# Places in a hand-written instruction order: similarities, sums, the fourth load, the low parts and the routing's ranks

## The chip, the cores and the metric

The kernel runs on one core of a Trainium2 chip. The metric is the device time of one execution in microseconds (us); the time of a kernel is the median of its runs. TensorE is called PE below, VectorE DVE, ScalarE ACT, GpSimd POOL and SyncE SP, as the profile does.

## The reference, cut to what matters

```python
# attention: q, k, v are (4 batches, 8 heads, 768 rows, 64)
q_assign = argmax(q_n @ c_n.T)          # nearest of 16 centroids, of normalized rows
k_assign = argmax(k_n @ c_n.T)
scores = (q @ k.T) / 8, where q_assign == k_assign, else -1e9
attn = exp(scores - max) / sum
x = (attn @ v) as 3072 tokens x 512
# routed experts: 8 of them, 512 -> 1024 -> 512
do_compute = x @ w_skip > 0
e = argmax(x @ w_gate); gate = softmax(x @ w_gate)[e]
out = x + gate * (relu(x @ w1[e]) @ w2[e])   # where do_compute, else out = x
```

## The kernel before, in words

Attention runs over 16 pairs of heads: 4 batches by 4 pairs, each pair two heads side by side. The experts follow, 8 in turn. Attention ends at about 460 us of the span, and the change lies in it alone.

The order of attention's instructions is written out by hand. `tasks` (L328) gives every step of pair i a time, counted in slots from that pair's first score. A pair has 24 slots (NS), one for each block of scores: two halves hf, six blocks kt, two heads a. `steps` (L305) takes the steps of all pairs off one heap by time, 24i + t, and issues them in that order; a step that yields a number goes back on the heap later by it, and one that yields a tuple waits for that time of its own pair. Each engine then runs its own instructions strictly in that program order. PLAN (L48) holds the times; FIRST (L61) and LAST, END (L77) replace some of them for the first and the last pairs. A time such as -46.95 is slot 1.05 of the pair two before; what follows names times by their slot in the running pair.

One slot holds, on PE, a score block (`score` L629: two products, L635 and L636) and a block of another pair's row maxima (`smax` L581: one product L586, whose maximum is taken by DVE at L588). ACT takes the exponential of the score block (L638), POOL adds exponentials up (L644, L650). Three times in a pair PE stops that rhythm for a group of products with v (`avs` L652, line L661, 16 records). These groups stand at slots 1.6, 9.6 and 17.6; below they and what follows them up to the next group are stretch A, B and C. During a group DVE has no new maxima to take, so its other work is put there: the choice of centroids, the low parts, the output's scaling and the routing.

The steps that the change moves:

- `sims` (L485): four products (L492) of 32 columns each with the centroids, then `assign` (L522) on DVE: a 32x32 transposition (L525), and in `first_max` (L502) a maximum (L506), a comparison (L509), a product with weights (L514), a maximum (L517) and an equality (L519), then a second transposition (L532). A yield stands between each two.
- `sums` (L695): four products (L701) of 32 columns that sum the exponentials, evicted by ACT (L704), then `recip` (L708: three transpositions L713, reciprocals L718) and `xout` (L789: three transpositions L764, then a scaling by DVE, L769, or ACT, L786).
- `load` (L393): the DMA of q and k of a pair into one of two buffers (RAW, by i % 2), on SP's queue. The buffer's last readers are the DMAs of `copies_lo` (L453, issued at L457) of the pair two before. SP also issues `load_v`, `gate_weights`, the copies of `split_hi` (L436), the mask rows (L555), the outputs (L778) and the experts' weights (L1300).
- `split_hi` (L429, ACT) and `split_lo` (L438, DVE L443): the high and low part of q (t = 0) and k (t = 1); `copies_lo` sends the low parts on at slots 2.8 and 2.9.
- `route_slots` (L864): after each of batches 0 to 2 (pairs 3, 7, 11), on DVE in small steps, the rank of each token within its expert: `route_c` (L957) with rk, rank, hi, los (L970 to L981), two one-hot tables oht (L985) and hs (L989), `route_cum` (L1011), then two products rhs and an accumulation in `route_d` (L993), then `route_e` (L1019). SLOTS (L58) lists the 20 times at which its yields wait.

PSUM has eight banks. `take` and `give` (L381, L390) hand them round in the order in which they were given back, so PE can run ahead of DVE and ACT only until the next bank in that order is still being read.

Of the kernel before, what the change touches and what calls it, by code (L numbers as in the profile page):

```python
# [25 lines left out]
HP = H // 2  # L26
# [19 lines left out]


PLAN = {  # L48
    "load": -60.0, "load_v": -45.0, "weights": 72.0, "sims": -46.95, "assign": (-46.42, 0.02, 0.02, 0.02, (-38.41,), 0.02),
    "hi": (-38.405, -38.40), "masks": (-32.5, 0.12), "lo": (-30.38, -30.37), "copies": (-22.1, -21.2, -21.1),  # L50
    "smax": (-21.6, 1.0, -0.2), "mneg": (-9.2, 4.0), "mrows": ((-6.5, 0.2, 0.05), (9.62, 0.1, 0.05)),
    "av": 1.6, "oT": (0.35, 3.55), "sums": 33.06, "recip": 33.64, "xout": (33.66, 49.55, 41.55),
    "route": (33.45, 41.5, 65.5), "early": (85.4, 100.9),
}

GATES = (41.62, 41.63, 41.64, 41.65, 41.66, 49.66, 49.67, 49.68, 49.69, 49.7, 49.71, 50.5,
         53.16, 53.17, 53.18, 65.67, 65.68, 65.69, 65.7, 73.66, 73.67)
SLOTS = (65.71, 65.72, 65.73, 65.74, 73.7, 73.71, 73.72, 73.73, 73.74, 81.66, 81.67, 84.4, 84.6,  # L58
         89.67, 89.68, 97.66, 97.67, 97.68, 97.69, 97.7)
CODES = {89.67: 85.9, 89.68: 85.91}  # L60
FIRST = {  # L61
    0: {
        "load_v": -18.9, "sims": -20.0, "hi": (-19.9, -19.8, -19.7, -19.6), "assign": (-19.0, 0.1, 0.01, 0.01, 0.01, 0.01),
# [6 lines left out]
        "mneg": (-4.6, 6.6), "mrows": ((-3.8, 0.2, 0.05), (9.45, 0.1, 0.05)),  # L70
    },
    2: {
        "load": -62.0, "load_v": -37.0, "sims": -38.9, "assign": (-38.42, 0.02, 0.02, 0.02, (-30.38,), 0.02), "hi": (-36.2, -30.3), "lo": (-22.39, -22.38), "masks": (-26.0, 0.12), "smax": (-17.6, 0.97, 0.0), "mneg": (-6.4, 5.2),
    },
}

LAST = {"sums": 29.2, "recip": 31.5, "xout": (31.52, 49.55, 37.55)}  # L77
# [5 lines left out]
class Kernel:  # L83
# [779 lines left out]

    def route_slots(self, i, bt):  # L864

        early = i == self.npair - HP - 1
        wait = iter([(CODES.get(t, t) if early else t,) for t in SLOTS])
        yield from self.route_c(i, bt * KT, KT, wait)
        yield next(wait)
        yield from self.route_cum(KT, wait)  # L870
        yield next(wait)
        yield from self.route_d(i, bt * KT, KT, wait=wait)
        yield next(wait)
        yield from self.route_e(i, bt * KT, KT, wait)
# [657 lines left out]
```

## Time and profile before

| what | us |
|---|---|
| median of 3 runs (lowest, highest) | 651.13 (650.85, 651.25) |
| the profiled execution's own time | 649.98 |
| its span | 648.3 |
| PE busy | 624.1, 96% of the span |
| DVE busy | 505.9, 78% |
| ACT busy | 410.0, 63% |
| POOL busy | 365.9, 56% |

Busy time of PE is modelled and its products overlap, so 96% says only that PE seldom stands still. What one more product costs is read from the chain of work that ended last: there a block of score or maxima stands with the time by which it moves the next one on.

### The profile page before, as it was taken

What the parts mean: (1) busy time and instruction counts of PE and PEld (TensorE: products, weight loads), DVE (VectorE), ACT (ScalarE), POOL (GpSimd) and SP (SyncE); (2) the same over time, 40 slices, a digit from 0 to 9 for tenths busy, and PEclk for the clock granted to TensorE, in tenths of its full rate; (3) what the DMA queues carried; (4) which work ended last, traced back from release to release, by engine and by line L of the source; (5) the groups of instructions that cost most, each with busy time, mean ns of one, the idle gap of its engine ahead of it and who ended that gap; (6) DMA issues with size and microseconds to landing.
All of it is one profiled execution on the core that took longest, in us unless ns stands there. A gap on an engine that the chain in (4) does not pass through costs nothing.

```text
span 648.3 us, 12165 instructions
## 1 busy us (share of the span) xinstructions
PE 624.1 (96%) x3873; PEld 460.5 (71%) x3873; DVE 505.9 (78%) x1060; ACT 410.0 (63%) x885; POOL 365.9 (56%) x384
## 2 busy tenths in 40 slices
PE   7879999999999999999999999999999999999994
PEld 3656776776667757767767666656799899899793
DVE  7967887888989869988888897885789766765721
ACT  7375787787767867867777777843654644645520
POOL 8784787777857867868777778631143212121101
PEclk9898999999999999999999999999999999999998
DMA  7396657776676565655754642341395766765711
GB/s 214 92 226 156 187 161 195 214 220 185 196 191 196 151 162 161 183 142 152 206 157 122 183 104 63 97 146 52 116 330 169 273 221 235 225 206 188 235 45 36
DMA packets 54322, 110.09 MB, mean 170 GB/s; under 512 B 8600, under 2 KB 22808, under 8 KB 54257
## 3 DMA queue, kind: packets, MB, share of 16 engines
q1 hardware_dynamic: 51232, 101.92, 54.2%
q0 software_dynamic: 2624, 7.18, 3.3%
q8 instruction: 32, 0.52, 0.3%
q14 instruction: 34, 0.27, 0.1%
q10 hardware_dynamic: 400, 0.20, 0.1%
HBM read 60.93 MB, written 10.55 MB: 110 GB/s over the span
## 4 chain that ended last, share of the span: by engine, by line
PE 67%; DMA 13%; issue 9%; DVE 8%; POOL 1%; ACT 1%; SPq 0%; POOLq 0%; DVEq 0%; ACTq 0%
PE ps L661 17%; PE ps L635 10%; PE ps L586 9%; PE ps L636 9%; DMA out<-yo,idw 7%; DMA raw<-qk 3%; DVE M L588 2%; PE ps L492 2%; PE ps L701 2%; DMA xg<-out,idr 2%; PE ph L1066 2%; PE ph L1065 2%; PE ph L1064 2%; PE ps L764 1%; DVE raw L443 1%
## 5 line engine op out<-in xcount | busy, mean ns | idle before, releaser
L650 POOL TENSOR_TENSOR acc<-acc,PT 128x384 f32<-128x384 f32 x246 | 245.6, 1027 | 43.8 <-ACT PT L638 43.0
L588 DVE TENSOR_REDUCE M<-ps 128x1 f32<-128x384 f32 x384 | 197.7, 552 | 38.6 <-PE ps L586 38.1
L638 ACT ACTIVATE PT<-ps 128x384 f32<-128x384 f32 x384 | 180.1, 492 | 42.1 <-PE ps L636 31.2
L635 PE MATMUL ps<-D 102*128 102x384 f32 x384 | 136.9, 356 | 4.5 <-DVE M L588 3.8
L661 PE MATMUL ps<-PT,vt 128*64 128x385 f32 x768 | 135.7, 494 | 0.0
L586 PE MATMUL ps<-D 96*128 96x384 f32 x384 | 133.4, 355 | 1.0 <-ACT D L566 1.0
L636 PE MATMUL ps<-D 128*128 128x384 f32 x384 | 130.4, 340 | 0.0
L661 PEld LDWEIGHTS ps<-PT,vt 128*64 128x64 f32 x768 | 50.8, 136 | 63.0 <-issue 60.1
L635 PEld LDWEIGHTS ps<-D 102*128 102x128 f32 x384 | 73.2, 191 | 25.7 <-issue 7.2
L644 POOL TENSOR_TENSOR acc<-PT 128x384 f32<-128x384 f32 x64 | 55.0, 878 | 61.0 <-ACT PT L638 60.3
L586 PEld LDWEIGHTS ps<-D 96*128 96x128 f32 x384 | 73.5, 192 | 22.1 <-ACT PT L638 8.7
L1222 POOL DMA_INDIRECT out<-yo,idw x15 | 20.3, 1350 | 111.9 <-DVE yo L1098 101.9
L636 PEld LDWEIGHTS ps<-D 128*128 128x128 f32 x384 | 73.6, 192 | 0.0
L1350 ACT ACTIVATE hh<-ph 128x256 fp32r<-128x256 f32 x56 | 21.5, 384 | 46.4 <-PE ph L1066 46.4
L1351 DVE SCALAR_TENSOR_TENSOR hl<-ph,hh 128x256 fp32r<-128x256 f32 x56 | 23.7, 423 | 33.6 <-ACT hh L1350 33.4
L1322 ACT ACTIVATE D<-wraw 128x1024 fp32r<-128x1024 f32 (+1 forms) x45 | 44.1, 1002 | 6.3 <-PE py L1066 4.7
L1064 PE MATMUL ph<-x2l,D 128*128 128x256 f32 x168 | 47.7, 284 | 0.0
L1065 PE MATMUL ph<-x2h,D 128*128 128x256 f32 x168 | 47.5, 283 | 0.0
L1064 PE MATMUL py<-D,hh 128*128 128x512 f32 x112 | 45.0, 402 | 0.0
L621 ACT ACTIVATE D<-ps,blocks 6x256 fp32r<-6x256 f32 x84 | 33.3, 457 | 16.1 <-PE ps L610 15.7
L1323 DVE TENSOR_TENSOR D<-wraw,D 128x1024 fp32r<-128x1024 f32 (+1 forms) x29 | 34.3, 1184 | 6.3 <-ACT D L1322 5.6
L443 DVE TENSOR_TENSOR raw<-raw,D 128x768 fp32r<-128x768 f32 x28 | 35.9, 1310 | 0.1
(312 smaller groups left out, 1032.0 us busy)
## 6 DMA issues: line engine op xcount, KB each, us to landing
wraw<-w SPq DMA_DIRECT2D x72, 512.0 KB, 4.9
D<-D SPq DMA_DIRECT2D x124, 192.0 KB, 3.4
raw<-qk SPq DMA_DIRECT2D x16, 768.0 KB, 5.7
D<-raw SPq DMA_DIRECT2D x60, 192.0 KB, 3.4
vt<-v SPq DMA_DIRECT2D x16, 384.0 KB, 4.1
out<-x SPq DMA_DIRECT2D x31, 192.0 KB, 2.8
D<-mk SPq DMA_DIRECT2D x120, 24.0 KB, 1.9
out<-yo,idw POOLq DMA_INDIRECT x15, 4.9
```

The costliest lines, as they stand in the source:

```text
L443: eng.tensor_tensor(out=lo.bitcast(F32R), in0=lo, in1=c[f"hi{t}"].bitcast(F32), op=ALU.subtract)
L586: nc.tensor.matmul(sm, lhsT=c["qm"][a][0:96, j * P:(j + 1) * P], rhs=c["kb"][a][0:96, hf * HALF:(hf + 1) * HALF], start=True, stop=True)
L588: nc.vector.tensor_reduce(out=c["m"][:, j, a, hf:hf + 1], in_=sm, axis=AX.X, op=ALU.max)
L635: nc.tensor.matmul(ps, lhsT=c["kb"][a][:MR, ks], rhs=c["qm"][a][:MR, sl], start=True, stop=False)
L636: nc.tensor.matmul(ps, lhsT=c["kc"][a][:, ks], rhs=c["qc"][a][:, sl], start=False, stop=True)
L638: nc.scalar.activation(out=pt, in_=ps, func=AF.Exp, scale=D ** -0.5)
L644: nc.gpsimd.tensor_tensor(out=acc, in0=self.pt(i, s - 2)[:, :HALF], in1=pt, op=ALU.add)
L650: (nc.vector if dve else nc.gpsimd).tensor_tensor(out=acc, in0=acc, in1=pt, op=ALU.add)
L661: nc.tensor.matmul(av[a * D:(a + 1) * D, :], lhsT=c["vt"][:, kt, a * D:(a + 1) * D], rhs=self.pt(i, hf * 2 * KT + kt * 2 + a), start=(kt = ...
L1064: mm(ps, lhsT=ah, rhs=bl, start=first, stop=False)
L1065: mm(ps, lhsT=ah, rhs=bh, start=False, stop=False)
L1322: nc.scalar.activation(out=h[:, cs], in_=r[:, cs], func=AF.Copy)
```

## The change

Nothing is added to the computation or taken from it; entries of the order are placed anew.

- `sims` goes from slot 1.05 to 1.52 (for pairs 3 to 15) and from 9.1 to 9.54 (pair 2): behind the maxima block of slot 1.2 (9.4 for pair 2), which stood between it and what follows.
- `sums` goes from slot 9.06 to 9.55, behind the maxima block of slot 9.4 (pairs 0 to 13; pair 14 has its own time).
- In `assign` the product with weights (L514) goes from stretch A to B for pairs 3 to 15, in front of the maximum L517. Pairs 0 to 2 keep their own lists.
- `split_lo` of k (t = 1) goes from slot 17.63, right behind that of q, to slot 1.62 of the next stretch A, for pairs 3 to 15.
- The load of pair 3 (the fourth) goes from slot 12 to slot 8 of the first pair.
- `route_slots`: rk, rank, hi and los go from stretch C to the next stretch A (65.71 to 73.69). After batches 0 and 1 the steps behind them move on too: oht, hs and cum from A to B, the second rhs from B to C, the accumulation from C's end to a later place in C, and the first two steps of `route_e` from C to A. After batch 2 those keep their places.

```diff
-    "load": -60.0, "load_v": -45.0, "weights": 72.0, "sims": -46.95, "assign": (-46.42, 0.02, 0.02, 0.02, (-38.41,), 0.02),
-    "hi": (-38.405, -38.40), "masks": (-32.5, 0.12), "lo": (-30.38, -30.37), "copies": (-22.1, -21.2, -21.1),
+    "load": -60.0, "load_v": -45.0, "weights": 72.0, "sims": -46.48, "assign": (-46.42, 0.02, 0.02, (-38.42,), 0.02, 0.02),
+    "hi": (-38.405, -38.40), "masks": (-32.5, 0.12), "lo": (-30.38, -22.38), "copies": (-22.1, -21.2, -21.1),
...
-    "av": 1.6, "oT": (0.35, 3.55), "sums": 33.06, "recip": 33.64, "xout": (33.66, 49.55, 41.55),
+    "av": 1.6, "oT": (0.35, 3.55), "sums": 33.55, "recip": 33.64, "xout": (33.66, 49.55, 41.55),
...
-SLOTS = (65.71, 65.72, 65.73, 65.74, 73.7, 73.71, 73.72, 73.73, 73.74, 81.66, 81.67, 84.4, 84.6,
-         89.67, 89.68, 97.66, 97.67, 97.68, 97.69, 97.7)
-CODES = {89.67: 85.9, 89.68: 85.91}
+SLOTS = ((73.69, 73.7, 73.71, 73.72, 81.67, 81.68, 81.69, 81.7, 81.71, 81.72, 89.66, 91.0, 91.2,
+          97.66, 97.67, 97.68, 97.69, 97.7, 97.71, 97.72),
+         (73.69, 73.7, 73.71, 73.72, 73.73, 73.74, 73.75, 73.76, 73.77, 81.66, 81.67, 84.4, 84.6,
+          85.9, 85.91, 97.66, 97.67, 97.68, 97.69, 97.7))
...
     2: {
-        "load": -62.0, "load_v": -37.0, "sims": -38.9, "assign": (-38.42, 0.02, 0.02, 0.02, (-30.38,), 0.02), "hi": (-36.2, -30.3), "lo": (-22.39, -22.38), "masks": (-26.0, 0.12), "smax": (-17.6, 0.97, 0.0), "mneg": (-6.4, 5.2),
+        "load": -62.0, "load_v": -37.0, "sims": -38.46, "assign": (-38.42, 0.02, 0.02, 0.02, (-30.38,), 0.02), "hi": (-36.2, -30.3), "lo": (-22.39, -22.38), "masks": (-26.0, 0.12), "smax": (-17.6, 0.97, 0.0), "mneg": (-6.4, 5.2),
     },
+    3: {"load": -64.0},
...
-        early = i == self.npair - HP - 1
-        wait = iter([(CODES.get(t, t) if early else t,) for t in SLOTS])
+        wait = iter([(t,) for t in SLOTS[i == self.npair - HP - 1]])
```

## Rows read from the trace of the kernel before

**Rows 1.** The page's first part: busy time, share of the span, instructions.
```profile
PE 624.1 (96%) x3873; PEld 460.5 (71%) x3873; DVE 505.9 (78%) x1060; ACT 410.0 (63%) x885; POOL 365.9 (56%) x384
```

**Rows 2.** Waits of PE, whole span: total us, times, longest us.
```profile
PE ps L492 <- DMA raw<-qk: 4.3, 2, 3.6
PE ps L635 <- DVE M L588: 3.8, 5, 1.1
```

**Rows 3.** Chain that ended last, 202 to 209 us, a stretch A: start, us, what.
```profile
203.13 0.78 PE ps L492 x8
203.92 0.38 PE ps L586
...
204.62 2.74 PE ps L661 x16
...
208.10 0.18 PE ps L635
```

**Rows 4.** The same chain, 209 to 219 us, the next stretch B.
```profile
211.63 0.78 PE ps L701 x8
212.41 0.37 PE ps L586
```

**Rows 5.** The same chain, 58 to 64 us: transpositions behind a group of v products.
```profile
62.43 0.48 PE ps L713 x3
62.91 0.33 PE ps L764 x3
```

**Rows 6.** The same chain, 0 to 66 us: the fourth load and what follows.
```profile
39.24 9.16 DMA raw<-qk
48.53 1.51 PE ps L492 x8
50.04 0.62 PE ps L586
50.66 3.36 PE ps L661 x16
```

**Rows 7.** Busy us of each engine by stretch; the figure behind POOL is PE's granted clock.
```profile
48.50:51.00 2.50, 2.47 (x11) 0.81 (x13) 0.30 (x1) 0.00 (x0) 0.00 (x0) 0.50 0.19 47
```

**Rows 8.** The DMAs of line L457, 28 to 45 us: issue times, and landing.
```profile
L457 SPq DMA_DIRECT2D D<-raw x4: 600/635/831, 32.2 to 34.5; - x4
...
DMA to landing us min/median/max: 3.8/4.0/4.3
```

**Rows 9.** The loads of line L396, 0 to 80 us: landing.
```profile
DMA to landing us min/median/max: 4.3/5.2/9.2
```

**Rows 10.** Timeline, 166 to 178 us, a stretch C with routing: start, us, engine, what.
```profile
169.24 2.63 DVE L443 TENSOR_TENSOR raw<-raw,D 128x768 fp32r<-128x768 f32 x2
...
173.16 0.20 DVE L970 TENSOR_TENSOR rk<-ps,ohd 128x48 f32<-128x48 f32 x1
...
174.04 0.91 DVE L981 SCALAR_TENSOR_TENSOR los<-hi,rank 128x6 f32<-128x6 f32 x1
...
175.47 0.45 PE L635 MATMUL ps<-D 102*128 102x384 f32 x1 [1.09 <-DVE M L588]
```

**Rows 11.** Timeline of DVE, 176 to 202 us, the stretches A and B behind it.
```profile
182.05 1.02 DVE L985 TENSOR_TENSOR oht<-iota,los 128x384 bf16<-128x384 f32 x2
...
183.33 0.62 DVE L1017 TENSOR_TENSOR cum<-cum,cs 128x8 bf16<-128x8 bf16 x1
...
190.24 0.77 DVE L999 TENSOR_TENSOR rhs<-rv,hs 128x240 bf16<-128x240 bf16 x2
...
191.22 0.27 DVE L718 RECIPROCAL rs<-ps 128x6 f32<-128x6 f32 x2 [0.20 <-PE ps L713]
```

**Rows 12.** Line L443, 166 to 260 us: duration ns min/median/max.
```profile
L443 DVE TENSOR_TENSOR raw<-raw,D x8: 947/1209/1762, 169.2 to 248.4; 128x768 fp32r<-128x768 f32 x8
```

**Rows 13.** Line L514, whole span: duration ns min/median/max.
```profile
L514 DVE TENSOR_TENSOR eqc<-eqc,wts x16: 552/557/560, 9.6 to 361.3; 128x384 f32<-128x384 f32 x16
```

**Rows 14.** Line L981, whole span: duration ns min/median/max.
```profile
L981 DVE SCALAR_TENSOR_TENSOR los<-hi,rank x5: 161/910/922, 174.0 to 446.8; 128x6 f32<-128x6 f32 x3, 128x3 f32<-128x3 f32 x2
```

## The prediction, made before the changed kernel was run

> **What bounds the kernel now.** I read the busy shares first: PE works 96% of the span [rows 1], so the question is what PE does with its time and where it stands still. The waits of PE answer the second part: it waits little, and two entries carry nearly all of it in attention, 4.3 us for a load of q and k (3.6 of it in one wait) and 3.8 us in five waits for DVE's maxima [rows 2]. The first part comes from the chain of work that ended last. In the steady rhythm it is PE's own stream, one product every 0.18 us [rows 3], so a slot of three products is 0.53 us. One thing breaks the stream beside the real work: a 128-column product that comes behind products of 32 columns moves the chain on by 0.38 or 0.37 us in place of 0.18 [rows 3, 4]. So PE is the bound, and a gain has to be a wait of PE or such a step; DVE matters only where it makes PE wait.
>
> **The fourth load.** The load of pair 3 is issued at 39.24 and lands 9.16 us later, at 48.40, and PE starts the similarities of pair 3 at 48.53 [rows 6], 3.57 of the 3.6 us wait [rows 2] after its previous product ended at 44.96. Behind the wait the granted clock is 0.50, that is 1.2 GHz [rows 7], after an engine that had stood still; the similarities take 1.51, the maxima block 0.62 and the v products 3.36 us [rows 6], against 0.78, 0.38 and 2.74 at full clock [rows 3], 1.59 us more. From 44.96 to the group's end at 54.02 are 9.06 us. With the load in time and the new order they are 0.18 + 0.78 + 2.74 = 3.70, so the whole wait is worth 5.4 us.
>
> Is it in time? The buffer is read by the low copies of pair 1; the last of the four is issued at 34.5 and lands at most 4.3 later, at 38.8 [rows 8]. Placed at slot 8, the load stands behind these copies on SP's queue and waits for that landing, so it is issued at 38.8 to 39.2, hardly sooner than now. What changes is what stands ahead of it: now two loads of v, the gate weights and two high copies are in flight, and 9.16 is the longest landing of five loads; the others take 4.3 to 5.2 and some more [rows 9]. I take 5.2, the median: landing at 44.0 to 44.4, against 45.1 when PE wants it. That is close, 0.7 us, and it is the step I trust least. Queued behind the waiting load on SP are the v loads of pairs 1 and 2 and the gate weights (wanted a stretch or more later) and the four high copies of pair 2, held for up to 3.6 us. Those are wanted by the first maxima of pair 2, some 2.4 us (4.4 slots) behind the v products, at 51; a stall of 0 to 1.5 us, of which I take 0.3. Sum: -5.0 us, between -5.4 and 0.
>
> **Sums.** Today they stand 32-column, 128-column (maxima), 64-column (v products), and the maxima block pays 0.37 [rows 4]. Behind the change the maxima block keeps the rhythm at 0.18 and the sums run straight into the v products. The v products take 2.74 behind a 128-column block, so entering column tiles shows no price. 14 pairs by 0.19 us = -2.7 us. The eviction L704 comes some 0.2 us later; nothing needs it before the transpositions behind the v products, 2.7 us on.
>
> **Similarities.** The same would hold, but in 12 of the 13 stretches A (pairs 4 to 15) three transpositions of `xout`, 128 columns wide, stand between slot 1.52 and the v products. Leaving column tiles then costs there: three transpositions behind v products take 0.48, three behind others 0.33 [rows 5], 0.15 more. So the gain is 0.20 - 0.15 = 0.05 by 12 = 0.6, and 0.2 for pair 2; that of pair 3 is in the load. -0.8 us. Bounds: 0.2 if the transpositions pay the full 0.20, and 12 by 0.20 + 0.2 = 2.6 if they pay nothing. The page TensorEngine Tiling (Array Packing) of the Trainium skill, Key Properties, says that a change of tiling mode drains PE; by it the number of changes in a stretch A is four before and four after, and this edit gives 0.2, not 0.8. The rows agree for leaving a mode and show no price for entering one.
>
> **The ranks and the low part, taken from stretch C.** There DVE works through two low parts (2.63 us), then the gates and, from 173.16 to 174.95, rk, rank, hi and los; the maxima come after that, and PE, having run out of free banks, waits 1.09 us [rows 10]. That wait stands once behind each of batches 0, 1 and 2, three of the five in [rows 2]. With one low part (1.3) and 1.8 us of ranks gone, DVE is free 3.1 us sooner, and nothing else is late: 3 by 1.09 = -3.3 us. In all other pairs stretch C makes PE wait for nothing and loses only a low part.
>
> **What that costs in stretches A and B.** In A the low part arrives, 0.95 to 1.76 us, median 1.21 [rows 12], and the product L514 leaves, 0.56 [rows 13]: about 0.65 more, and DVE gets its similarities some 0.5 sooner, since the maxima block is no longer behind them. The cover is the v products and, behind them, four slots that PE can run ahead on free banks, 2.74 + 4 x 0.53 = 4.9 us, and the list (transposition, maximum, comparison, low part, the first maxima) is some 3.5 us. No price in the pairs without routing. Behind batches 0 and 1, A gains the ranks too (0.7 to 1.8 us, as los takes 161 to 922 ns [rows 14]) but loses oht, hs and cum, from 182.05 to 183.95, 1.9 us [rows 11]; there the two small waits of PE that are left of the five, 0.5 us in all [rows 2], go or stay. I take them as gone, -0.5, with +1 as the other end. The GPSIMD Engine Reference of the Trainium skill, Specifications, says that GpSimd shares SBUF interfaces with VectorE; by it los is short where POOL is idle, as it is under v products, and the ranks cost 0.7 in A. The 161 and 922 of one small shape agree with that.
>
> B takes 0.56 (L514) in every pair: in front of it DVE waits for PE at the maxima block, which comes 0.6 sooner now; no price. Behind batches 0 and 1, B also takes oht, hs and cum, 1.9, and gives up one rhs of two, 0.4 [rows 11]: 0.56 + 1.9 - 0.4 = 2.1 us ahead of the reciprocals, whose bank PE wants two slots after the transpositions. Against it stand 0.2 us that DVE waits there now [rows 11], the 0.5 by which it starts sooner and two slots, 1.1: 1.8 in all. A stall of 0.3 by this, 0 to 1.9 by its ends; I take 0.5, twice: +1.0. One PSUM bank (rk's input) is held eight slots longer in three stretches; with six others left the rhythm needs no more.
>
> **Sum.** -5.0 - 2.7 - 0.8 - 3.3 - 0.5 + 1.0 = -11.3 us on the profiled execution's own 649.98, that is 638.7. The median of the runs lies 1.15 above that execution, so 639.8. PE's stream goes on to the end of the span, and nothing there is tied to a clock of its own, so I pass the whole of it on.
>
> **The rivals.**
> 1. The load is late all the same. For it: its issue hardly moves, and 9.16 is a landing that the trace shows. Against: that one had several transfers ahead of it. From 39 + 9.2 = 48.2 PE waits 3 us of the 3.6 again, clock included; the gain of the load is 0 to 1. Time 644 to 645. Chance 0.15.
> 2. Every switch of mode drains, entering too, as the tiling page has it: then similarities give 0.2 and the sums as forecast, 640.4. Chance 0.1. The opposite, where transpositions pay nothing and B shows no stall, is 637. Chance 0.07.
> 3. Slower: PE's run-ahead on free banks is not there in the steady pairs, and DVE's list decides stretch A. Place: the first maxima behind the v products; it decides from the point at which that list passes 4.9 us. Price: the low part in full (1.3) less L514 (0.56), 0.75, and L514 in B, 0.56, by 12 pairs = 15.7, with up to 3.8 in B behind routing; C gives nothing back, since PE doesn't wait there. With 12.3 of gains that is +7, 658. Against it: PE waits for DVE in no stretch A without routing now. Chance 0.05.
> 4. The order does not show: DVE's new waits eat what the switches give and the load is late: 650 to 652. Chance 0.04.
>
> **How the numbers follow.** Forecast 639.8, chance 0.59; with the parts of rival 2 the band 637 to 642 holds 0.76. The range goes from all terms at their better end (-5.4, -2.8, -2.6, -3.3, -0.5, no stall: 636.5) to a late load, 645.5. About 0.2% (1.3 us) is what a measurement of this kernel tells from none. Faster 0.91, same 0.04, slower 0.05.
>
> **What would show it.** Among PE's waits the load's 3.6 us is gone, and the clock's 0.50 behind it; the three waits of 1.1 for the maxima are gone. In the chain, L586 takes 0.18 in front of sums and similarities, L661 follows L701 directly, and the first transpositions behind L492 take about 0.48. Wrong it would be by a new wait: L492 or the first maxima of pair 2 on a DMA at 45 to 52 us, or L635 on DVE's reciprocals, scaling or maxima in A and B.

## The result, and the profile after

The changed kernel takes 642.74 us (median; 641.93 to 643.25) against 650.99: ratio 0.9872, interval 0.9855 to 0.9889. It is 8.2 us faster, inside the forecast range, where 11.3 us of gain were forecast. Its profiled execution has a span of 640.2 us against 648.3.

The lines of the kernel's code stand one or two lower than before (L637 is the former L635, L588 the former L586). First the changed kernel's busy shares and PE's waits for DVE from 40 us on; the columns are those of [rows 1] and [rows 2].

```profile
PE 619.7 (97%) x3873; PEld 459.1 (72%) x3873; DVE 504.1 (79%) x1060; ACT 409.3 (64%) x885; POOL 361.9 (57%) x384
```
```profile
PE ps L637 <- DVE M L590: 2.7, 1, 2.7
...
PE ps L588 <- DVE rs L720: 0.5, 2, 0.3
...
PE ps L637 <- DVE x L771: 0.5, 2, 0.2
```

The wait for the load is gone, and so are the five for the maxima, 3.8 us. In their place stands one wait of 2.7 us for the maxima, and four small ones for the reciprocals and the output's scaling. The steady stretches look as forecast. The chain of work that ended last, 288 to 335 us, a stretch A and then the next stretch B (start, us, what):

```profile
296.20 0.17 PE ps L588
296.38 0.78 PE ps L494 x8
297.16 0.48 PE ps L766 x3
...
304.64 0.17 PE ps L588
304.81 0.78 PE ps L703 x8
305.59 2.74 PE ps L663 x16
```

The maxima block L588 takes 0.17 where it took 0.38 and 0.37 [rows 3, 4]; the sums run straight into the v products; behind the similarities the transpositions take 0.48, not 0.33 [rows 5].

Where the time went is read from the starts of the v products in the two timelines, us:

```
group of v products                     before    after   difference
first                                    29.48    29.44    -0.04
third, behind the similarities of 3      50.59    45.79    -4.80
fourth                                   59.62    54.01    -5.61
batch 0: stretch C begins               169.00   162.44    -6.56
         stretch A begins               179.10   170.88    -8.22
         stretch B begins               187.78   178.84    -8.94
         next stretch C begins          196.06   187.89    -8.17
batch 2: stretch C begins               375.55   364.44   -11.11
         stretch A begins               384.68   371.95   -12.73
         stretch B begins               392.82   383.89    -8.93
         next stretch C begins          401.16   392.74    -8.42
end of the span                         648.28   640.17    -8.11
```

At 372 us the change is 12.7 us ahead, more than forecast. In the stretch A that follows batch 2 and in its wake it gives 4.3 of them back. PE and DVE there, from the timeline of the changed kernel (start, us, engine, what; in brackets idle time and what ended it):

```profile
372.20 1.59 DVE L445 TENSOR_TENSOR raw<-raw,D 128x768 fp32r<-128x768 f32 x1
373.72 0.97 DVE L951 CAST vals<-g 128x6 bf16<-128x6 f32 x1
...
375.63 0.17 DVE L982 SCALAR_TENSOR_TENSOR los<-hi,rank 128x6 f32<-128x6 f32 x1
375.83 1.70 DVE L986 TENSOR_TENSOR oht<-iota,los 128x384 bf16<-128x384 f32 x2
377.45 0.82 DVE L990 TENSOR_TENSOR hs<-iota,hi 128x12 bf16<-128x12 f32 x1
...
378.45 0.76 DVE L1018 TENSOR_TENSOR cum<-cum,cs 128x8 bf16<-128x8 bf16 x1
379.14 1.01 DVE L590 TENSOR_REDUCE M<-ps 128x1 f32<-128x384 f32 x2
...
379.74 0.44 PE L637 MATMUL ps<-D 102*128 102x384 f32 x1 [2.67 <-DVE M L590]
```

Between the last maxima of the stretch before (ended 372.28) and the first new ones (379.14) DVE has 6.9 us of low part, gate values, ranks and tables to do. The v products start at 371.95 and PE works through four slots behind them, to 377.1; then its banks are used up. The 6.9 us and 0.6 of the first new maxima, against the 4.8 from 372.28 to 377.07, make the wait of 2.67. The stretch 382 to 384 us shows the clock behind the wait at 0.50, 1.2 GHz (busy us by engine, then the granted clock):

```profile
382.00:384.00 2.00, 2.00 (x12) 0.33 (x13) 1.99 (x4) 0.51 (x2) 2.00 (x3) 0.50 0.00 0
384.00:387.00 3.00, 3.00 (x16) 1.11 (x16) 1.12 (x2) 2.38 (x3) 0.85 (x1) 0.84 0.03 5
```

### The profile page after: what moved, and what is told of

The parts are those of the page before. It is cut to its first block, busy times and chain, and to the rows that moved or that the text cites. A ratio compares the mean times of both kernels' runs of the same rounds, so it can differ in the third digit from the quotient of the medians.

```text
span 640.2 us, 12142 instructions
## 1 busy us (share of the span) xinstructions
PE 619.7 (97%) x3873; PEld 459.1 (72%) x3873; DVE 504.1 (79%) x1060; ACT 409.3 (64%) x885; POOL 361.9 (57%) x384
## 4 chain that ended last, share of the span: by engine, by line
PE 31%; DMA 10%; issue 9%; DVE 4%; ACT 0%; POOL 0%; POOLq 0%; DVEq 0%
DMA out<-yo,idw 7%; PE ps L663 6%; PE ps L637 4%; PE ps L638 3%; PE ps L588 3%; DMA xg<-out,idr 2%; PE ph L1066 2%; PE ph L1065 2%; PE ph L1067 2%; PE py L1066 1%; PE py L1065 1%; PE py L1067 1%; DVE M L590 1%; DMA PT<-out,idr 1%; PE ps L703 1%
## 5 line engine op out<-in xcount | busy, mean ns | idle before, releaser
L652 POOL TENSOR_TENSOR acc<-acc,PT 128x384 f32<-128x384 f32 x246 | 242.2, 1013 | 47.3 <-ACT PT L640 46.9
L637 PE MATMUL ps<-D 102*128 102x384 f32 x384 | 135.9, 354 | 3.9 <-DVE M L590 2.7
L588 PE MATMUL ps<-D 96*128 96x384 f32 x384 | 130.3, 346 | 2.2 <-ACT D L568 1.0
L637 PEld LDWEIGHTS ps<-D 102*128 102x128 f32 x384 | 72.8, 190 | 24.5 <-issue 6.6
L588 PEld LDWEIGHTS ps<-D 96*128 96x128 f32 x384 | 73.1, 191 | 6.3 <-ACT D L568 1.4
L1065 PE MATMUL py<-D,hh 128*128 128x512 f32 x112 | 45.0, 402 | 0.0
L623 ACT ACTIVATE D<-ps,blocks 6x256 fp32r<-6x256 f32 x84 | 33.3, 457 | 12.7 <-PE ps L612 12.3
L1066 PE MATMUL py<-D,hh 128*128 128x512 f32 x84 | 33.0, 392 | 0.0
```

The source lines that it names most:

```text
L588: nc.tensor.matmul(sm, lhsT=c["qm"][a][0:96, j * P:(j + 1) * P], rhs=c["kb"][a][0:96, hf * HALF:(hf + 1) * HALF], start=True, stop=True)
L637: nc.tensor.matmul(ps, lhsT=c["kb"][a][:MR, ks], rhs=c["qm"][a][:MR, sl], start=True, stop=False)
L652: (nc.vector if dve else nc.gpsimd).tensor_tensor(out=acc, in0=acc, in1=pt, op=ALU.add)
L1065: mm(ps, lhsT=ah, rhs=bl, start=first, stop=False)
L1066: mm(ps, lhsT=ah, rhs=bh, start=False, stop=False)
```

## The experiments

The differences in us inside a trace are differences of the starts of v products, as in the table above, against the changed kernel unless said otherwise. The kernel before ran beside each, and ratios are to it. All of them compute the whole result. Line numbers are each kernel's own: L493 of the kernel with the load back is L492 of the kernel before.

**The load back** (`load_back`).

```diff
-    3: {"load": -64.0},
```

> The changed kernel with the load of pair 3 back at slot 12, all else as changed. My account: the wait of PE for that load returns in front of L494 with the slow clock behind it, 5.3 us, so 648.0 (ratio 0.9955). Rival, that the load's wait was mostly covered by something else and the gain came from the order around it: less than 2 us, so under 644.7.

Measured: 647.95 us, ratio 0.9958 (0.9935 to 0.9982), against 0.9872 with the load moved. PE's wait is back:

```profile
PE ps L493 <- DMA raw<-qk: 3.1, 1, 3.1
```

The load lands 8.8 us behind its issue here (at 39.23) and 4.4 us behind it in the changed kernel (at 39.03). There SP issued nothing from 34.9 us up to the load; here it issued two loads of v, two of the gate weights and two high copies in that time. Up to 372 us this kernel is 4.8 us behind, so more than half of the 8.2 us that the change gives is this one transfer. A further 1.2 us come behind batch 2, where the clock stays low for longer behind the same wait (last section); that the median meets the expected 648.0 is in part chance.

**The load alone** (`load_alone`), in the kernel before.

```diff
+    3: {"load": -64.0},
```

> The kernel before with the load of pair 3 at slot 8 and nothing else. My account: PE's wait for it goes with its slow clock, 4.8 us (what putting it back cost in the trace) to 5.3: ratio 0.992, 645.9. Rival, that the load is only in time because the similarities of pair 3 stand later: some of the wait stays, 646.5 or more, and a wait of L492 for raw shows in the trace.

Measured: 644.98 us, ratio 0.9922 (0.9892 to 0.9953), 4.9 us in the trace by 60 us and unchanged to the end. No wait of L492 for raw is left. So the load doesn't need the later similarities.

**The sums back** (`sums_back`).

```diff
-    "sums": 33.55,
+    "sums": 33.06,
```

> The changed kernel with the sums back at slot 9.06, in front of the maxima block. My account: the maxima block pays the 0.19 us for leaving 32-column products again in 14 stretches B, 2.7 us, so 645.4 (ratio 0.9914), and PE's chain shows 0.37 for it. Rival, that PE's stream is not what sets the time in stretch B: under 1 us more, below 643.7.

Measured: 645.72 us, ratio 0.993 (0.9908 to 0.9951). The trace is 2.86 us behind at 372 us, near 14 x 0.19 = 2.7, and another 1.5 behind the wait of stretch A. That wait is 2.7 us here too, but the clock behind it stays low for longer (last section), so the 1.5 are not the sums'. The chain of this kernel, 300 to 312 us, shows the price where it was expected:

```profile
306.84 0.78 PE ps L703 x8
307.62 0.37 PE ps L588
307.99 2.74 PE ps L663 x16
```

**The similarities back** (`sims_back`).

```diff
-    "sims": -46.48, ...   (pair 2: -38.46)
+    "sims": -46.95, ...   (pair 2: -38.9)
```

> The changed kernel with the similarities back at slot 1.05 (9.1 for pair 2). My account: 0.05 us in each of 12 stretches A and 0.2 for pair 2 and for pair 3, 1.0 us, so 643.7 (ratio 0.989). Rival by the tiling rule, that each change of mode costs the same: 0.4 us, 643.1, within what can be told; the chain then shows the same sum of L494, L588 and the transpositions as in the changed kernel.

Measured: 644.59 us, ratio 0.992 (0.9891 to 0.9949); the trace is 2.73 us behind at 372 us, more than either account gives. 0.9 of it are small steps, about 0.05 in a stretch A and 0.5 by pairs 2 and 3 (0.3 of that stands at the first group already, where traces of kernels that are alike so far differ by up to 0.15): the chain, 290 to 300 us, has 0.38 + 0.33 behind L494 where the changed kernel has 0.17 + 0.48.

```profile
298.12 0.78 PE ps L494 x8
298.91 0.38 PE ps L588
299.28 0.33 PE ps L766 x3
```

The other 1.8 are three steps of 0.6, in the stretch A in which the gates of a batch are worked out, and there a wait shows that the changed kernel has not:

```profile
PE ps L588 <- DVE M L590: 1.0, 3, 0.4
```

Similarities behind the maxima let DVE start its list sooner, and in three stretches that decides whether PE waits. The kernel before has the similarities at the same early place and no wait there; its low part of k stands in stretch C, and with that moved alone a wait of 0.5 to 0.7 us comes there (`low_alone`). The forecast had the effect (0.5 us sooner) and no price for it.

**The tables behind batch 2 moved to stretch B** (`tables_to_b`).

```diff
-         (73.69, 73.7, 73.71, 73.72, 73.73, 73.74, 73.75, 73.76, 73.77, 81.66, 81.67, 84.4, 84.6,
+         (73.69, 73.7, 73.71, 73.72, 81.61, 81.62, 81.63, 81.64, 81.65, 81.66, 81.67, 84.4, 84.6,
```

> The changed kernel with oht, hs and cum behind batch 2 moved from stretch A (73.73 to 73.77) to stretch B (81.61 to 81.65). My account of the new wait of 2.67 us at 379.7: DVE's list there runs 6.9 us from the last maxima to the next ones, past the 4.9 us that the v products and four slots of run-ahead cover; without the tables (3.3 us) the list is 3.6 and the wait is gone with its slow clock, 4.2 us less: 638.5 (ratio 0.981), with up to 1 us of a new wait in stretch B. Rival, that PE lacks a PSUM bank since rk's input is held eight slots longer: the list is not the cause, the wait stays, 642.7.

Measured: 637.53 us, ratio 0.9799 (0.9773 to 0.9826). The wait of 2.7 us is gone from the list, which now has

```profile
PE ps L588 <- DVE rs L720: 0.6, 2, 0.3
PE ps L637 <- DVE x L771: 0.5, 2, 0.3
```

and the trace is 4.4 us ahead of the changed kernel. rk's input holds its bank as long as in the changed kernel, so the bank was not the cause.

**The last pair's low part back in stretch C** (`last_low_back`).

```diff
-END = {"mrows": ...
+END = {"lo": (-30.38, -30.37), "mrows": ...
```

> The changed kernel with the low part of k of the last pair alone back in stretch C. It takes 1.59 us out of DVE's list behind batch 2. By the list account the wait of 2.67 us falls to some 1.1, and with a shorter gap the clock may stay: 1.6 to 3 us less, 639.7 to 641.1. By the rival (a missing PSUM bank) nothing changes, 642.7.

Measured: 637.66 us, ratio 0.9804 (0.9778 to 0.9831); 4.1 us ahead in the trace, more than expected. 1.6 us less of work took 2.4 us off the wait, of which 0.3 is left. The rest of the list became 0.8 us shorter in sum: oht 1.03 where it took 1.70, hs 0.16 where it took 0.82 (below), against rv, 1.04 where it took 0.31.

```profile
374.78 1.03 DVE L986 TENSOR_TENSOR oht<-iota,los 128x384 bf16<-128x384 f32 x2
375.72 0.16 DVE L990 TENSOR_TENSOR hs<-iota,hi 128x12 bf16<-128x12 f32 x1
```

This run shows one thing more. In its stretch C behind batch 2 both low parts stand again and only the ranks are gone, and PE does not wait there: the starts around that stretch lose 0.1 us against the changed kernel.

```profile
364.54 2.62 DVE L445 TENSOR_TENSOR raw<-raw,D 128x768 fp32r<-128x768 f32 x2
...
368.46 3.80 DVE L590 TENSOR_REDUCE M<-ps 128x1 f32<-128x384 f32 x8
```

**The ranks and tables of all batches back** (`ranks_back`), the low part left where the change put it.

```diff
-SLOTS = ((73.69, 73.7, 73.71, 73.72, 81.67, 81.68, 81.69, 81.7, 81.71, 81.72, 89.66, 91.0, 91.2,
-          97.66, 97.67, 97.68, 97.69, 97.7, 97.71, 97.72),
-         (73.69, 73.7, 73.71, 73.72, 73.73, 73.74, 73.75, 73.76, 73.77, 81.66, 81.67, 84.4, 84.6,
+SLOTS = ((65.71, 65.72, 65.73, 65.74, 73.7, 73.71, 73.72, 73.73, 73.74, 81.66, 81.67, 84.4, 84.6,
+          89.67, 89.68, 97.66, 97.67, 97.68, 97.69, 97.7),
+         (65.71, 65.72, 65.73, 65.74, 73.7, 73.71, 73.72, 73.73, 73.74, 81.66, 81.67, 84.4, 84.6,
```

> The changed kernel with all of the routing's ranks and tables at their old times, and the low part of k where the change put it. It tells which of the two moves took the three waits of 1.09 us out of stretch C. If the low part alone does (1.3 us out of a list that overran by 1.1): no wait in C, the 2 x 0.8 us of new small waits in B gone, the wait behind batch 2 cut by the ranks' 0.75 us to 1.9: 642.7 - 1.6 - 0.8 = 640.3. If the ranks were needed: up to 3 x 1.1 us of waits in C return: 643.6.

Measured: 637.04 us, ratio 0.9811 (0.9776 to 0.9846), 5.0 us ahead of the changed kernel in the trace, of which 0.5 stands behind each of batches 0 and 1 and the rest behind batch 2. That is some 3 us better than expected: the wait behind batch 2 was put at 1.9 us, and 0.26 is left. Stretch C has no wait for the maxima at all: with one low part in front of them the ranks are done at 166.4 and the maxima go on at once (timeline of DVE, 160 to 180 us; before it was 174.95 in a stretch that began 6.6 us later).

```profile
166.27 0.17 DVE L982 SCALAR_TENSOR_TENSOR los<-hi,rank 128x6 f32<-128x6 f32 x1
166.35 3.85 DVE L590 TENSOR_REDUCE M<-ps 128x1 f32<-128x384 f32 x8
```

So the low part alone is enough to take the three waits out of stretch C, and with it moved, the move of the ranks and tables brought nothing there and cost 5 us. The kernel with the last pair's low part back shows the other half behind batch 2: there the ranks' move alone is enough.

**The low part alone** (`low_alone`), in the kernel before.

```diff
-    ... "lo": (-30.38, -30.37), ...
+    ... "lo": (-30.38, -22.38), ...
```

> The kernel before with the low part of k at slot 1.62 and nothing else. My account after the runs so far: this alone takes the three waits of 1.09 us out of stretch C, 3.3 us; in stretch A the product with weights stays too, so behind the routing up to 0.6 us of small waits come in each of three: 1.5 to 3.3 us less than the kernel before, 647.8 to 649.6 (ratio 0.995 to 0.9977). Rival, that the ranks have to leave stretch C as well: no gain, 651.

Measured: 658.53 us, ratio 1.0132 (1.0097 to 1.0166): slower by 1.3%, where both accounts had it at or below the kernel before. Stretch C does lose its wait, 1.6 us each time. But in stretch A the list is now longer than its cover: the product with weights L514 is still there, the similarities still stand in front of the maxima block, and behind each batch the tables stand there too:

```profile
PE ps L635 <- DVE M L588: 7.0, 6, 2.5
...
PE ps L701 <- POOL acc L650: 2.0, 3, 0.7
```

Against the kernel before, the stretch A of the gates loses 1.5 to 1.7 us in each of three batches and that of the tables 2.2 behind batch 0 and 4.8 behind batch 1. The step that takes three times 1.6 us out of stretch C is a net loss of 8 to 9 by itself. With the ranks back the tables and the low part share stretch A as well, and behind batches 0 and 1 that kernel loses only 0.5 us each time against the changed one. That leaves the later similarities and the move of L514 as what makes room for the low part; no run shows what L514 alone is worth.

**The output's transpositions in front of the similarities** (`out_first`).

```diff
-    "xout": (33.66, 49.55, 41.55),
+    "xout": (33.66, 49.5, 41.55),
```

> The changed kernel with the output's transpositions (L766) moved in front of the similarities (slot 1.55 to 1.50), so that 32-column products run straight into the v products in stretch A. My account: the first of three transpositions then no longer pays 0.15 us for leaving column tiles, 12 times, 1.8 us less: 641.0 (ratio 0.9845). Rival, that a block behind a switch costs the same wherever it is put: no change, 642.7.

Measured: 639.98 us, ratio 0.9847 (0.9815 to 0.9879). In front of the v products of each of the 12 stretches A it gains some 0.15 us in the trace, the mechanism as expected; chain, 290 to 310 us:

```profile
295.39 0.33 PE ps L766 x3
295.72 0.78 PE ps L494 x8
296.50 2.74 PE ps L663 x16
```

In two stretches A with the gates it loses 0.6, since the similarities reach DVE 0.33 us later and PE waits for the maxima there. 0.9 us are left at 372 us. A further 1.6 come behind batch 2, where PE waits the same 2.7 us and the clock doesn't fall (last section); they are not the edit's own.

**Two combinations**: the tables in B with the transpositions first (`best`), and the ranks back with the transpositions first (`best2`).

> The changed kernel with both edits that gained: oht, hs and cum behind batch 2 in stretch B, and the output's transpositions in front of the similarities. By the sum of the two, against the changed kernel 4.4 us (tables) and 0.9 us (transpositions, up to the wait that the tables remove): 637.4, with 636.5 by the runs' own medians. Rival, that the two share a gain: 637.5 as with the tables alone.

> The changed kernel with the ranks and tables of the routing at their old times and the output's transpositions in front of the similarities. By the sum of the spans against the changed kernel: 5.0 us for the ranks, 0.7 for the transpositions (net of two new small waits): 1.0 us under the kernel with the ranks back alone. Rival, that the small waits in stretch A grow, since the similarities come 0.33 us later for DVE: no gain over it.

Measured: 635.99 us, ratio 0.9794 (0.976 to 0.9828), and 636.25, ratio 0.9789 (0.9756 to 0.9821) with the shortest span of all, 633.4. Both are faster than the changed kernel, by 5.1 and 5.6 us in the trace; which of the two is the better can't be told, nor whether the transpositions add anything to what tables_to_b and ranks_back reach alone, since the intervals overlap.

## Why the prediction was right, and where it was not

The sign and the range held, and the view held that PE's own stream is the bound. The sum came out 3.1 us too good because one term was left out. That it came so near is in part luck: at 372 us the change was 1.4 us better than the whole forecast, since the waits in stretch C were worth more than they were put at, and the term left out then took 4.3.

- **The load**: forecast -5.0, measured 4.8 and 4.9 us (load_back, load_alone). The landing was the weakest step; it took 4.4 us, quicker than the 5.2 taken. The stall at the first maxima of pair 2 didn't come. Rival 1, a late load, is out.
- **The sums**: forecast -2.7; 2.86 in the trace. Right by its mechanism.
- **The similarities**: forecast -0.8; the kernel with them back is 2.7 behind, pair 3 included. The switching steps are the forecast ones, 0.17 and 0.48 in place of 0.38 and 0.33, and come to 0.9. The other 1.8 are no gain on the kernel before, which has no wait in those stretches [rows 2]: they are what the low part would cost in the stretches with the gates if DVE did not start 0.5 us sooner. The forecast's "no price in the pairs without routing" held there only by that. Rival 2, that all switches cost the same, does not fit: entering column tiles is free behind L588 (0.17) and behind L766 (0.33 in front of the v products) alike. By the time alone it could not be told from the forecast.
- **Stretch C**: forecast 3 x 1.09; measured 1.7, 1.7 and 1.6 by the starts (from C to A; the table has the first and the last). The waits did go, and each had cost more than the 1.09 named. In the kernel before PE's products start 1.42 us apart at the wait, where 0.18 is the rhythm, the next one comes 0.1 late, and a small stall stands in front that the list of waits does not name:

```profile
173.08 0.33 PE L636 MATMUL ps<-D 128*128 128x384 f32 x1
173.41 0.44 PE L586 MATMUL ps<-D 96*128 96x384 f32 x1
...
174.05 0.33 PE L586 MATMUL ps<-D 96*128 96x384 f32 x1
```

  The prediction gave the cause to the two moves together; ranks_back shows that the low part alone is enough, and last_low_back that behind batch 2 the ranks alone are.
- **A and B behind batches 0 and 1**: forecast -0.25 and +0.5 for each. The table has -0.72 in A behind batch 0, of which 0.2 are the sums', and +0.77 in B; a further 0.2 comes in the next C. B's stall stands where it was put, at the reciprocals and the scaling. As a rough estimate from these runs, 4.8 + 2.9 + 0.9 + 5.0 - 0.9 = 12.7 us, which is what the table has at 372 us.
- **A behind batch 2**: forecast nothing, measured +4.3. This is the step that failed. The prediction priced the ranks' arrival in stretch A "behind batches 0 and 1" and took batch 2's wait in C as pure gain, although the diff keeps oht, hs and cum in stretch A there, so that low part, ranks and tables all meet. By rows at hand, a low part of 1.3, ranks of 0.7 to 1.8 and tables of 1.9 [rows 10 to 12, 14] come with the gate values (0.5 and more) to an estimate of 4.5 to 6 us, and the first maxima (0.6) stand behind them, against a cover of 4.9: the trace of before gave a list at or over the edge, and it was not added up. What actually ran was 6.9 us and the 0.6. tables_to_b took the tables out of the list and the wait was gone; last_low_back took 1.6 out and the wait fell to 0.3.

Rival 3, DVE deciding stretch A, was given 0.05 in the changed kernel. Its mechanism is what happens when the low part is moved by itself (low_alone), and in one stretch of the changed kernel, but in the stretches with the gates and the routing and not in the steady pairs where the rival placed it: those lose nothing in either kernel. The cover of 4.9 us was read rightly; what was not read is how near the lists stood to it.

Why the parts of the list behind batch 2 took longer than their rows is read from the timelines: they ran beside POOL. It was not tested by an edit of POOL's work alone. In the changed kernel POOL adds exponentials (start, us) from 368.53 to 374.65 and again from 375.92 to 380.02:

```profile
368.53 6.12 POOL L652 TENSOR_TENSOR acc<-acc,PT 128x384 f32<-128x384 f32 x6 [1.22 <-ACT PT L640]
375.92 2.33 POOL L646 TENSOR_TENSOR acc<-PT 128x384 f32<-128x384 f32 x2 [1.26 <-ACT PT L640]
378.21 1.81 POOL L652 TENSOR_TENSOR acc<-acc,PT 128x384 f32<-128x384 f32 x2
```

The low part (1.59) and vals (0.97) fall into the first stretch, oht, hs and cum into the second; rk to los, at 0.17 to 0.20 each, stand in the 1.3 us between them. In the kernel before the same three tables ran while POOL stood still, from 385.21 to 388.64:

```profile
385.58 1.02 DVE L985 TENSOR_TENSOR oht<-iota,los 128x384 bf16<-128x384 f32 x2
386.52 0.16 DVE L989 TENSOR_TENSOR hs<-iota,hi 128x12 bf16<-128x12 f32 x1
...
388.64 1.68 POOL L644 TENSOR_TENSOR acc<-PT 128x384 f32<-128x384 f32 x2 [3.43 <-ACT PT L638]
```

In the kernel with the tables in B they run beside POOL from end to end, and take the longest:

```profile
377.49 6.03 POOL L652 TENSOR_TENSOR acc<-acc,PT 128x384 f32<-128x384 f32 x6
...
379.63 2.21 DVE L986 TENSOR_TENSOR oht<-iota,los 128x384 bf16<-128x384 f32 x2
381.76 0.97 DVE L990 TENSOR_TENSOR hs<-iota,hi 128x12 bf16<-128x12 f32 x1
```

The prediction took the short value for A because POOL is idle under the v products. Behind batch 0 of the changed kernel it is, from 171.94 on, 1.1 us behind their start, and the low part takes 1.07 there:

```profile
166.53 5.41 POOL L652 TENSOR_TENSOR acc<-acc,PT 128x384 f32<-128x384 f32 x6 [1.22 <-ACT PT L640]
```

Behind batch 2 stretch C is 0.9 us shorter (364.44 to 371.95, against 162.44 to 170.88): no later pair's similarities stand in it. POOL works to 374.65, as good as to the end of the v products. It starts again as soon as PE's new blocks have passed ACT. So the list met POOL at both ends, and the wait grew with it.

## What to carry to other kernels

Where an engine's side work hides under a fixed block of the bound engine, add up the whole list for every place where the block stands, the rare ones first, and compare it with the block plus the run-ahead that free banks allow; a move that is harmless in twelve places can cost in the thirteenth. Moves that share such a block are not separable: test them alone and together, as the same low part takes three waits away in one order and is a loss of 1.3% in the other. A transfer that lands late may need another place in its queue and not an earlier issue: here it was issued at the same time and landed in half the time.

## What the runs showed of the hardware that was not expected

- The same small DVE operation takes 0.16 to 0.2 us or 0.8 to 1.0, and in the timelines read here the long values stand beside POOL's exponentials: hs 0.16 and 0.82, vals 0.17 to 0.97. The prediction had such a spread for los alone [rows 14].
- A wait of one length has different prices. Behind batch 2 PE waits 2.7 us in the changed kernel and in the ones with the load, the sums or the similarities back and with the transpositions first. Behind that wait the granted clock is 0.50 for a while in the changed kernel (shown above), for longer with the load, the sums or the similarities back (still 0.50 from 387 to 389 us), and not at all with the transpositions first; so it cost 2.7 us and nothing to some 3 us more. The rows are of the kernel with the sums back, then of the one with the transpositions first (busy us by engine, then the granted clock):

```profile
383.00:385.00 2.00, 2.00 (x7) 2.00 (x7) 1.60 (x6) 0.81 (x2) 0.65 (x1) 0.50 0.00 0
385.00:387.00 2.00, 2.00 (x9) 1.19 (x12) 1.05 (x2) 1.07 (x3) 1.90 (x3) 0.50 0.00 0
```
```profile
379.00:381.00 2.00, 2.00 (x12) 1.90 (x12) 2.00 (x6) 1.37 (x3) 0.93 (x2) 1.00 0.00 0
381.00:383.00 2.00, 2.00 (x18) 0.68 (x18) 2.00 (x4) 1.45 (x4) 2.00 (x4) 1.00 0.00 0
```

The kernel with the low part alone has both in one execution: waits of 2.46 us at 187.8 and 2.47 us at 293.2, the clock at 1.00 behind the first and 0.50 behind the second, and 2.2 against 4.8 us lost. What decides between the two was not found out. A kernel's median holds this, so two kernels that keep such a wait are compared by the trace up to it.
